# Weight sums, forms of x and squares in a two-MLP kernel: where the splits are made and what holds the buffers

## The chip, the cores and the metric

The kernel runs on one core of a Trainium2 chip. The metric is the device time of one execution in microseconds (us); before the change it is 1036.32 us, the median of two runs (1035.69 and 1036.94). The engines are named as in the profile: PE is TensorE (PEld its weight loads), DVE is VectorE, ACT is ScalarE, POOL is GpSimd and SP is SyncE, which only issues transfers here.

## What is computed

Sparse attention (half of the heads local, half strided), and then two MLPs one after the other, on 2304 tokens of 512 features:

```python
attn_out = _attn_ref(q, k, v)                       # 4 batches, 8 heads, 576 positions, 64 wide
x = transpose(attn_out).reshape(2304, 512)
h = x @ w_in;  r = np.maximum(h, 0.0)               # first MLP, 2048 wide
x = (s * (r * r) + b) @ w_out
a = x @ w2_a;  b2 = x @ w2_b                        # second MLP, 1536 wide
out = (a * b2) @ w2_out
```

Weights come as 64-bit words that have to be made float32 on the core.

## The kernel before

Every float32 operand is *split* into a high and a low half in a matmul format: ScalarE copies the high half, VectorE subtracts it from the value and writes the low one. Each product then is three matmuls (high by high, high by low, low by high).

**First MLP.** The tokens are taken in five blocks, n = 0 to 4, of 512, 384, 512, 384 and 512 columns. A block goes through 16 slices f of the hidden layer: h_mm makes h (12 matmuls), ScalarE writes r = relu(h) and squares it in place, split makes gt, and o_mm (12 matmuls) adds to the block's output, which leaves as o1s to DRAM at the block's end. The attention of the next block runs inside blocks 0 to 3.

**Second MLP.** It goes over the tokens in three pairs (0, 1, 2) of two 384-column blocks, and takes seven products instead of eight per 2 x 2 block of matrices. For this it needs sums and differences of the weight's quarters (s1 to s4 beside a11, a12, a22) and of x's quarters (the *forms* b11, b22, t1, t3, t2, b21, t4, two tiles each). A pair is 12 groups g of seven products (42 matmuls a group, "pp<-x2w,wf"), whose results become quads, and then a second-layer stage of 42 steps of six matmuls ("o<-gf,o2w"), where gf is the split of a quad's part.

**Work for the second MLP that lies elsewhere.** convert_w2 takes the 36 weight tiles through blocks 1 to 3: a load into raw, the conversion to w2s, a write of the whole tile to DRAM (w2d), splits of those quarters that need no sum, back into raw, and their writes to w2a, w2b and w2o from POOL's queue. raw is free again when that write has landed. sums(g) loads two such tiles again (w2r, four tiles), makes s1 to s4 (w2t), splits them (w2z, w2t) and writes them to w2s or w2o; there are 18, 15 of them emitted in block 4 and the last three within the first groups of pair 0. The forms of pair 0 are made in block 4 straight into the x2w tiles. Those of pairs 1 and 2 are made during the products of the pair before them, in two staging tiles (x2s), written to DRAM (x2d) from POOL's queue and copied back to x2w by SP in the second-layer stage.

**What sets the order.** Each engine runs its own instructions in program order, with what a scheduler has put there at build time. The helpers act and dve (L611 and L616) tie their calls into a chain on ScalarE and on VectorE. A transfer waits in its queue until its source is written and its destination is free, and those behind it in that queue wait too. SP's queue holds the loads wf (four per group, six tiles), w2r, o2w (eight tiles), xr and the copies x2w. Tiles of a pool come free with the last reader of their former contents.

Of the kernel before, what the change touches and what calls it, by code (L numbers as in the profile page):

```python
# [2 lines left out]

# [16 lines left out]
P = 128  # L20
# [6 lines left out]
def sparse_attention_two_mlps(  # L27
# [66 lines left out]
    FORMS = ("b11", "b22", "t1", "t3", "t2", "b21", "t4")  # L94
    x2d = [
        {name: [dram.tile([P, 2, TB2], F32, name=f"x2d{i}{name}{kk}") for kk in range(2)] for name in FORMS}
        for i in range(1, NP2)
    ]
# [38 lines left out]
    def to_float32(r, out=None, quarters=False):  # L137
# [12 lines left out]
        if quarters:  # L150
            to = out.rearrange("p (a i c) -> p a i c", a=2, c=STR)
            low, high = (t.rearrange("p (i a c) -> p a i c", a=2, c=STR) for t in (low, high))
            pieces_ = [(to[:, a], high[:, a], low[:, a]) for a in range(2)]
# [625 lines left out]
    def h_mm(n, f):  # L779
# [11 lines left out]
        with tc.high_priority(offset=URGENT):  # L791
            r = hp.tile([P, TM], F32, tag="r", name="r")[:, 0:T]
            relu = nc.scalar.activation(out=r, in_=ph, func=AF.Relu)  # L793
            gt = gp.tile([P, 2, TM], F32R, tag="gt", name="gt")
            hi, lo = gt[:, 0, 0:T], gt[:, 1, 0:T]
            nc.scalar.activation(out=r, in_=r, func=AF.Square)  # L796
            last = split(hi, lo, r)
            if n == 1:
                nc.scalar.activation(out=gt[:, :, T:T + 2], in_=bc, func=AF.Copy)
# [28 lines left out]
    def halves_of(w):  # L828
        return w.rearrange("p (a r c) -> p r a c", a=2, c=P)

    def convert_w2():
        words = {}
        for i in range(3 * NF2 + 1):
# [3 lines left out]
            if i:  # L837
                f, kind = divmod(i - 1, 3)
                with after(list(behind)):
                    r = words.pop(i - 1)  # L840
                    w = to_float32(r, hp.tile([P, DM], U32, tag="w", name="w2s"), kind == 2)
                    nc.gpsimd.dma_start(out=w2d[i - 1], in_=w)  # L842
                    z = r.rearrange("p c t -> p (c t)").bitcast(F32R)
                    if kind < 2 and f % 2 == 0:
                        z = z.rearrange("p (e c) -> p e c", e=2)
                        split(z[:, 0], z[:, 1], w)
                        to = w2a[f + kind]
                    elif kind < 2:
                        z = z[:, 0:DM].rearrange("p (e c) -> p e c", e=2)
                        split(z[:, 0], z[:, 1], w[:, HALF:])  # L850
                        to = w2b[f - 1 + kind]
                    elif f % 2 == 0:
                        z = z[:, 0:DM].rearrange("p (e a c) -> p e a c", e=2, a=2)
                        split(z[:, 0], z[:, 1], halves_of(w)[:, 0])
                        z = z.rearrange("p e a c -> p e (a c)")
                        to = w2o[f // 2][:, 0]
                    else:
                        z = z.rearrange("p (r e a c) -> p r e a c", r=2, e=2, a=2)
                        split(z[:, :, 0], z[:, :, 1], halves_of(w))
                        z = z.rearrange("p r e a c -> p r e (a c)")  # L860
                        to = w2o[f // 2][:, 1:3]
                    nc.gpsimd.dma_start(out=to, in_=z.bitcast(F32))
# [4 lines left out]
    NQ2 = NF2 // 2  # L867

    def sums(g, chained=False):
        if g < NG2:  # L870
            pair, kind = divmod(g, 2)
            first_, second = 6 * pair + kind, 6 * pair + 3 + kind
        else:
            first_, second = 6 * (g - NG2) + 2, 6 * (g - NG2) + 5
        r = [p2.tile([P, DM], F32, tag="r", name="w2r", bufs=4) for _ in range(2)]
        for t, i in zip(r, (first_, second)):
            nc.sync.dma_start(out=t, in_=w2d[i])
        yield
        t = p2.tile([P, 4, HALF], F32, tag="s", name="w2t", bufs=2)
        z = p2.tile([P, 4, HALF], F32R, tag="z", name="w2z")  # L880
        s2, s1, s3, s4 = (t[:, i] for i in range(4))
        vector = partial(dve, "tensor_tensor") if chained else nc.vector.tensor_tensor
        if g < NG2:
            a11, a12 = r[0][:, 0:HALF], r[0][:, HALF:]
            a21, a22 = r[1][:, 0:HALF], r[1][:, HALF:]
        else:
            a11, a21 = (halves_of(r[0])[:, i] for i in range(2))
            a12, a22 = (halves_of(r[1])[:, i] for i in range(2))
            s2, s1, s3, s4 = (i.rearrange("p (a c) -> p a c", a=2) for i in (s2, s1, s3, s4))
# [8 lines left out]
        for e, src in enumerate((z, low)):  # L898
            if g < NG2:
                nc.gpsimd.dma_start(out=w2s[g][:, :, e], in_=src.bitcast(F32).rearrange("p (i r) c -> p i (r c)", i=2))  # L900
            else:
                nc.gpsimd.dma_start(out=w2o[g - NG2][:, 3:, e], in_=src.bitcast(F32))  # L902
# [57 lines left out]
    def x2_forms(xr, pair):  # L960
        b11, b12, b21, b22 = (xr[:, c, 2 * r:2 * r + 2] for r in range(2) for c in range(2))

        def less(out_, in0, in1):
            dve("tensor_tensor", out=out_, in0=in0, in1=in1, op=ALU.subtract)
# [467 lines left out]
```

## Time and profile before

| what | us |
|---|---|
| median of two runs | 1036.32 |
| the profiled execution | 1035.28 |
| its span in the trace | 1033.6 |
| PE busy in it | 918.0 |
| DVE busy | 641.6 |
| ACT busy | 413.2 |
| POOL busy | 147.0 |
| moved by DMA | 241.33 MB |

The profile is of one execution. An engine is busy while it runs an instruction; waits for semaphores and the issue of transfers are not counted. Times within the trace run from the start of its span. The attention alone and the first blocks take up to 147 us, blocks 1 to 3 reach to about 428 us, block 4 to 523, pair 0 to 720, pair 1 to 894, pair 2 to the end.

### The profile page before, as it was taken

What the parts mean: (1) busy time and instruction counts of PE and PEld (TensorE: products, weight loads), DVE (VectorE), ACT (ScalarE), POOL (GpSimd) and SP (SyncE); (2) the same over time, 40 slices, a digit from 0 to 9 for tenths busy, and PEclk for the clock granted to TensorE, in tenths of its full rate; (3) what the DMA queues carried; (4) which work ended last, traced back from release to release, by engine and by line L of the source; (5) the groups of instructions that cost most, each with busy time, mean ns of one, the idle gap of its engine ahead of it and who ended that gap; (6) DMA issues with size and microseconds to landing.
All of it is one profiled execution on the core that took longest, in us unless ns stands there. A gap on an engine that the chain in (4) does not pass through costs nothing.

```text
span 1033.6 us, 17448 instructions
## 1 busy us (share of the span) xinstructions
PE 918.0 (89%) x6274; PEld 832.0 (80%) x6274; DVE 641.6 (62%) x1313; ACT 413.2 (40%) x876; POOL 147.0 (14%) x292
## 2 busy tenths in 40 slices
PE   8999999989798998999959965869996578999997
PEld 7778888977676888988848855859996578999997
DVE  6898955546565666368537644845555385465594
ACT  6777754545444545565422211322121133111251
POOL 5000001111111111022211011006101101500002
PEclk9999999989998999999979987989998898999999
DMA  9858436676767675479899766899776599877666
GB/s 247 233 165 222 103 113 185 183 185 203 198 196 195 215 218 183 157 246 306 283 374 356 271 219 219 289 348 288 248 251 212 211 331 308 276 248 249 197 210 198
DMA packets 206246, 241.33 MB, mean 233 GB/s; under 512 B 110992, under 2 KB 152528, under 8 KB 206160
## 3 DMA queue, kind: packets, MB, share of 16 engines
q1 hardware_dynamic: 184400, 181.88, 58.0%
q0 software_dynamic: 18048, 57.42, 15.2%
q10 hardware_dynamic: 3712, 0.92, 0.5%
q8 instruction: 50, 0.82, 0.4%
q14 instruction: 36, 0.29, 0.1%
HBM read 177.24 MB, written 62.91 MB: 232 GB/s over the span
## 4 chain that ended last, share of the span: by engine, by line
issue 44%; PE 33%; DMA 9%; POOL 8%; DVE 3%; ACT 2%; SPq 1%; POOLq 0%; ACTq 0%
PE o L103 10%; PE pp L103 9%; PE h L103 5%; PE acc L103 5%; DMA o2w<-w2o 3%; POOL w2s L900 2%; POOL w2d L842 1%; POOL out_dram L1254 1%; DMA w2b<-raw 1%; DVE quad L616 1%; DMA x2w<-x2d2t 1%; DMA x2w<-x2d1t 1%; POOL w2o L902 1%; DMA x2w<-x2d2b 1%; PE fpo L103 1%
## 5 line engine op out<-in xcount | busy, mean ns | idle before, releaser
L103 PE MATMUL pp<-x2w,wf 128*128 128x384 f32 x1512 | 288.3, 351 | 55.6 <-ACT quad L611 29.0
L103 PEld LDWEIGHTS pp<-x2w,wf 128*128 128x128 f32 x1512 | 277.8, 199 | 65.7 <-ACT quad L611 31.2
L103 PE MATMUL h<-x,w 128*128 128x512 f32 (+1 forms) x960 | 227.2, 387 | 10.5 <-ACT r L793 9.1
L103 PE MATMUL acc<-gt,w 128*128 128x512 f32 (+2 forms) x960 | 212.7, 370 | 2.7 <-ACT gt L120 1.4
L103 PEld LDWEIGHTS h<-x,w 128*128 128x128 f32 x960 | 178.8, 196 | 38.4 <-ACT r L793 11.7
L103 PEld LDWEIGHTS acc<-gt,w 128*128 128x128 f32 x960 | 176.5, 189 | 27.3 <-ACT gt L120 2.2
L103 PE MATMUL o<-gf,o2w 128*128 128x384 f32 x756 | 136.9, 342 | 24.6 <-DMA o2w<-w2o 24.0
L103 PEld LDWEIGHTS o<-gf,o2w 128*128 128x128 f32 x756 | 134.6, 192 | 26.5 <-issue 24.7
L121 DVE TENSOR_TENSOR gt<-r,gt 128x512 fp32r<-128x512 f32 (+1 forms) x80 | 50.9, 636 | 79.8 <-ACT gt L120 79.5
L616 DVE TENSOR_TENSOR quad<-pp,quad 128x384 f32<-128x384 f32 x108 | 59.9, 555 | 57.2 <-PE pp L103 53.0
L611 ACT ACTIVATE gf<-quad 128x384 fp32r<-128x384 f32 x126 | 62.1, 521 | 80.4 <-PE o L103 59.2
L616 DVE TENSOR_TENSOR gf<-quad,gf 128x384 fp32r<-128x384 f32 x126 | 65.6, 551 | 25.4 <-ACT gf L611 25.0
L1254 POOL DMA_DIRECT2D out_dram<-ot x84 | 47.2, 570 | 212.3 <-DVE ot L1241 210.0
L793 ACT ACTIVATE r<-h 128x512 f32<-128x512 f32 (+1 forms) x80 | 44.3, 554 | 78.4 <-PE h L103 64.3
L611 ACT ACTIVATE quad<-pp 128x384 f32<-128x384 f32 x36 | 17.6, 489 | 125.0 <-PE pp L103 120.1
L139 ACT ACTIVATE raw<-raw 128x512 f32<-128x512 f32 x66 | 43.1, 677 | 54.7 <-DMA raw<-in_moe_w_a_dram 22.0
L611 ACT ACTIVATE x2s<-xr 128x384 fp32r<-128x384 f32 x28 | 14.0, 520 | 94.8 <-DMA x2d2t<-x2s 19.4
L120 ACT ACTIVATE gt<-r 128x512 fp32r<-128x512 f32 (+1 forms) x80 | 47.0, 587 | 1.6
L842 POOL DMA_DIRECT2D w2d<-w2s x36 | 19.7, 547 | 192.7 <-DVE w2s L155 160.9
L796 ACT ACTIVATE r<-r 128x512 f32<-128x512 f32 (+1 forms) x80 | 46.7, 583 | 0.7
L616 DVE TENSOR_TENSOR x2s<-xr,x2s 128x384 fp32r<-128x384 f32 x28 | 15.5, 554 | 47.8 <-ACT x2s L611 47.8
L142 DVE TENSOR_SCALAR raw<-raw 128x512 uint32<-128x512 uint32 x66 | 26.8, 424 | 29.3 <-DMA raw<-in_moe_w_a_dram 17.7
(168 smaller groups left out, 885.0 us busy)
## 6 DMA issues: line engine op xcount, KB each, us to landing
wf<-w2s SPq DMA_DIRECT2D x72, 512.0 KB
o2w<-w2o SPq DMA_DIRECT2D x126, 256.0 KB
wf<-w2a SPq DMA_DIRECT2D x36, 512.0 KB
raw<-in_moe_w_out_dram SPq DMA_DIRECT2D x28, 512.0 KB
w2d<-w2s POOLq DMA_DIRECT2D x36, 256.0 KB, 3.1
w2r<-w2d SPq DMA_DIRECT2D x36, 256.0 KB
wf<-w2b SPq DMA_DIRECT2D x36, 256.0 KB
raw<-in_moe_w_in_dram SPq DMA_DIRECT2D x16, 512.0 KB
```

Of the source, the lines that this page charges most:

```text
L103: last_pe[:] = [nc.tensor.matmul(*args, **kwargs).ins]
L120: nc.scalar.activation(out=hi, in_=src, func=AF.Copy)
L121: return nc.vector.tensor_tensor(out=lo, in0=src, in1=hi.bitcast(F32), op=ALU.subtract)
L139: nc.scalar.activation(out=high.bitcast(F32), in_=high.bitcast(F32), func=AF.Copy, scale=HIGH_SCALE)
L142: nc.vector.tensor_scalar(out=low, in0=low, scalar1=29, scalar2=None, op0=ALU.logical_shift_right)
L611: i = nc.scalar.activation(**kwargs).ins
L616: i = getattr(nc.vector, method)(**kwargs).ins
L793: relu = nc.scalar.activation(out=r, in_=ph, func=AF.Relu)
L796: nc.scalar.activation(out=r, in_=r, func=AF.Square)
L842: nc.gpsimd.dma_start(out=w2d[i - 1], in_=w)
L900: nc.gpsimd.dma_start(out=w2s[g][:, :, e], in_=src.bitcast(F32).rearrange("p (i r) c -> p i (r c)", i=2))
L1254: engines[i % len(engines)].dma_start(out=at.rearrange("(j t) c -> t j c", t=STR), in_=st[i * STR:(i + 1) * STR, j:j + m].rearrange("t j a ...
```

## The change

1. convert_w2 converts and writes w2d only. The splits of the quarters and their 30 writes leave blocks 1 to 3.
2. sums makes them, in block 4 and pair 0: it splits the sums (w2t) and also the loaded tiles (w2r), the high halves into a new tile spare, the low ones in place, and issues six writes instead of two. Thirteen sums are emitted from f = 2 of block 4 on, one for each f, the others in groups 0 to 4 of pair 0.
3. In blocks 1 to 3 h_mm lets ScalarE square straight into the high half, while VectorE squares r itself and subtracts.
4. Forms of x are made straight in the x2w tiles for all pairs: in a pair one bias for each of groups 3 to 10 and the first difference in group 11, ten of the fourteen copies in the second-layer stage (one every fourth step), and the last four in the first group of the next pair. The staging tiles, x2d and the copies back are gone.
5. Homes: twelve tiles for gf instead of eleven, of which two forms per quad are made during the products and the others eleven steps ahead instead of nine; o2w has two tiles of its own, two in the first MLP's room hp and four in w2r's; the next pair's first four wf loads stand in the second-layer stage instead of in group 11; the quads come last in the order of pools.

```diff
@@ h_mm
-            nc.scalar.activation(out=r, in_=r, func=AF.Square)
-            last = split(hi, lo, r)
...
+            if n in (0, NB - 1):
+                nc.scalar.activation(out=r, in_=r, func=AF.Square)
+                last = split(hi, lo, r)
+            else:
+                nc.scalar.activation(out=hi, in_=r, func=AF.Square)
...
+                nc.vector.tensor_tensor(out=r, in0=r, in1=r, op=ALU.mult)
+                last = nc.vector.tensor_tensor(out=lo, in0=r, in1=hi.bitcast(F32), op=ALU.subtract)
@@ convert_w2
-                    r = words.pop(i - 1)
-                    w = to_float32(r, hp.tile([P, DM], U32, tag="w", name="w2s"), kind == 2)
-                    nc.gpsimd.dma_start(out=w2d[i - 1], in_=w)
-                    z = r.rearrange("p c t -> p (c t)").bitcast(F32R)
-                    if kind < 2 and f % 2 == 0:
-                        z = z.rearrange("p (e c) -> p e c", e=2)
-                        split(z[:, 0], z[:, 1], w)
-                        to = w2a[f + kind]
...
-                    nc.gpsimd.dma_start(out=to, in_=z.bitcast(F32))
+                    w = to_float32(words.pop(i - 1), hp.tile([P, DM], U32, tag="w", name="w2s"), kind == 2)
+                nc.gpsimd.dma_start(out=w2d[i - 1], in_=w)
@@ sums
+    EARLY = NF1 - 3
...
-        (act if chained else nc.scalar.activation)(out=z, in_=t, func=AF.Copy)
-        low = t.bitcast(F32R)
-        vector(out=low, in0=t, in1=z.bitcast(F32), op=ALU.subtract)
...
+        if own:
+            forms = [(flat(t), 2, w2s[g]), (r[0], 1, w2a[g][:, None]), (a22, 1, w2b[g][:, None])]
+        else:
+            to = w2o[g - NG2]
+            forms = [(flat(t), 4, to[:, 3:]), (r[1], 2, to[:, 1:3]), (a11, 1, to[:, 0:1])]
+        z = [room(0), room(1)]
+        z = [z[0], z[1][:, 0:DM], z[1][:, DM:DM + HALF]]
+        for high, (src, _, _) in zip(z, forms):
+            scalar(out=high, in_=src, func=AF.Copy)
+            vector(out=src.bitcast(F32R), in0=src, in1=high.bitcast(F32), op=ALU.subtract)
+        for high, (src, m, to) in zip(z, forms):
+            for e, half in enumerate((high.bitcast(F32), src)):
+                nc.gpsimd.dma_start(out=to[:, :, e], in_=half.rearrange("p (i c) -> p i c", i=m))
@@ x2_forms, form
-                if pair:
-                    w = p2.tile([P, 2, DM], F32R, tag="s", name="x2s", bufs=2)
-                else:
-                    w = slot(wpa, [P, 2, DM], "x2w", F32R)
-                    fixed.append(w)
+                if len(fixed) < 2:
+                    fixed.append(slot(wpa, [P, 2, DM], "x2w", F32R))
+                w = fixed[kk]
...
-                if pair:
-                    nc.gpsimd.dma_start(out=x2d[pair - 1][name][kk], in_=w[:, :, 0:TB2].bitcast(F32))
@@ block 4
-                    next(added[f])
-                    if f:
-                        next(added[f - 1])
+                    if 0 <= f - 2 < EARLY:
+                        next(added[f - 2])
+                    if f == 3:
+                        spare = xp[1].tile([P, 3, 2 * DM], F32R, tag="x", name="spare")
+                    if 0 <= f - 3 < EARLY:
+                        next(added[f - 3])
@@ pools of the second MLP
-    gq, wf, tmp, rp, op = pool("gq", NQ2), pool("wf", 4), pool("tmp", 6), pool("rp", 8), pool("op", 4)
+    rp, op, wf, tmp, gq = pool("rp", 9), pool("op", 2), pool("wf", 4), pool("tmp", 6), pool("gq", NQ2)
@@ pair, groups
-                for _ in range(2):
-                    next(later_x[0], None)
-            elif later_x:
-                next(later_x[1], None)
+            if later_x and 3 <= g < 11:
+                next(later_x[0])
+            if later_x and g == 11:
+                next(later_x[1])
...
-            if pair == 0 and g + NF1 <= NG2 + NQ2:
-                if g + NF1 < NG2 + NQ2:
-                    next(added[g + NF1])
-                next(added[g + NF1 - 1])
+            j = EARLY + g
+            if pair == 0 and j < NG2 + NQ2:
+                if j + 1 < NG2 + NQ2:
+                    next(added[j + 1])
+                next(added[j])
@@ second-layer stage
-            if i >= 2 and copies:
-                name, kk = copies.pop(0)
-                nc.sync.dma_start(out=x2[name][kk][:, :, 0:TB2].bitcast(F32), in_=x2d[pair][name][kk])
+            if not last:
+                if i % 4 == 2 and 8 <= i < 24:
+                    next_room()
+                if i % 4 == 3:
+                    next(later_x[1])
```

**How the instructions move.** The first place is ScalarE in a middle block, where raw is the second MLP's weight in conversion, r and gt are the first MLP's hidden values. Before:

```order
L139 ACTIVATE raw<-raw 128x512
L796 ACTIVATE r<-r 128x512
L120 ACTIVATE gt<-r 128x512
L120 ACTIVATE x<-po 128x128 x2
L120 ACTIVATE raw<-w2s 128x2x256
L793 ACTIVATE r<-h 128x512
L139 ACTIVATE raw<-raw 128x512
L796 ACTIVATE r<-r 128x512
L120 ACTIVATE gt<-r 128x512
L120 ACTIVATE raw<-w2s 128x512
```

ScalarE in a middle block after the change:

```order
L135 ACTIVATE raw<-raw 128x512
L796 ACTIVATE gt<-r 128x512
L789 ACTIVATE r<-h 128x512
L135 ACTIVATE raw<-raw 128x512
L796 ACTIVATE gt<-r 128x512
L482 ACTIVATE pT<-ppt 128x256
```

The copies raw<-w2s are gone, and one instruction, gt<-r, stands where two stood.

The second place is the start of pair 0's products, on ScalarE (quad and u are the copies that TensorE waits for, w2z and spare the high halves of weights). Before:

```order
L820 ACTIVATE o1s<-acc,sb 128x512 x2
L895 ACTIVATE w2z<-w2t 128x1024
L611 ACTIVATE quad<-pp 128x384 x2
L611 ACTIVATE w2z<-w2t 128x1024
L611 ACTIVATE u<-pp 128x384
L611 ACTIVATE w2z<-w2t 128x1024
L611 ACTIVATE quad<-pp 128x384 x2
```

ScalarE at the start of pair 0's products after the change:

```order
L607 ACTIVATE quad<-pp 128x384 x2
L873 ACTIVATE spare<-w2t 128x1024
L873 ACTIVATE spare<-w2r 128x512
L873 ACTIVATE spare<-w2r 128x256
L873 ACTIVATE spare<-w2r 128x512
L873 ACTIVATE spare<-w2r 128x256
L873 ACTIVATE spare<-w2t 128x1024 x2
L873 ACTIVATE spare<-w2r 128x512
L873 ACTIVATE spare<-w2r 128x256
L607 ACTIVATE spare<-w2t 128x1024
L607 ACTIVATE gf<-w2r 128x512
L607 ACTIVATE gf<-w2r 128x256
```

The next row there is u<-pp of group 1: the splits of four sums stand ahead of it now (gf<-w2r is a high half in a tile that gf gets later). SP's queue in groups 1 and 2 after the change (w2s_167 holds the sums of group 2, its first load s2 and s1, its second s3 and s4):

```order
L908 DMA wf<-w2s_167 128x1024
L908 DMA wf<-w2b_155 128x2x256
L852 DMA w2r<-w2d_136 128x512
L852 DMA w2r<-w2d_139 128x512
L852 DMA w2r<-w2d_107 128x512
L852 DMA w2r<-w2d_110 128x512
L852 DMA w2r<-w2d_113 128x512
L852 DMA w2r<-w2d_116 128x512
L852 DMA w2r<-w2d_119 128x512
L852 DMA w2r<-w2d_122 128x512
L1180 DMA o2w<-w2o_177 128x512
L908 DMA wf<-w2s_167 128x1024
```

Before, two w2r loads stood among the wf loads of these groups; now the eight loads of four sums stand ahead of the second load of group 2.

The third place is SP's queue in pair 0's second-layer stage. Before:

```order
L1398 DMA x2w<-x2d1t_187 128x2x384
L933 DMA wf<-w2s_165 128x1024
L1398 DMA x2w<-x2d1t_188 128x2x384
L933 DMA wf<-w2a_142 128x1024
L1398 DMA x2w<-x2d1b_185 128x2x384
L933 DMA wf<-w2s_166 128x1024
L1398 DMA x2w<-x2d1b_186 128x2x384
L1210 DMA o2w<-w2o_179 128x512
L1398 DMA x2w<-x2d1t_195 128x2x384
L1210 DMA o2w<-w2o_180 128x512
```

SP's queue in pair 0's second-layer stage after the change:

```order
L908 DMA wf<-w2b_153 128x2x256
L908 DMA wf<-w2s_165 128x1024
L908 DMA wf<-w2a_142 128x1024
L908 DMA wf<-w2s_166 128x1024
L1180 DMA o2w<-w2o_179 128x512
L1180 DMA o2w<-w2o_180 128x512
L1180 DMA o2w<-w2o_181 128x512
```

The copies x2w<-x2d are gone from between the loads.

## Rows read from the trace of the kernel before

**Rows 1.** Windows of the second MLP; columns from start to GB/s as headed.

```profile
core 0: us, PE busy (x) PEld busy (x) DVE busy (x) ACT busy (x) POOL busy (x), PEclk, DMA share, GB/s
523.00:660.00 137.00, 102.82 (x508) 97.50 (x507) 70.41 (x133) 28.39 (x56) 15.50 (x22) 0.88 0.79 279
660.00:720.00 60.00, 46.33 (x254) 45.16 (x253) 35.90 (x69) 17.12 (x35) 14.10 (x26) 0.91 0.98 334
720.00:837.00 117.00, 96.00 (x503) 93.07 (x502) 62.14 (x118) 23.98 (x51) 17.47 (x29) 0.93 0.70 233
837.00:894.00 57.00, 46.13 (x255) 45.84 (x255) 36.28 (x70) 17.13 (x35) 13.08 (x24) 0.91 0.96 324
894.00:983.00 89.00, 88.55 (x504) 86.74 (x503) 52.44 (x99) 13.53 (x29) 5.01 (x9) 1.00 0.70 232
983.00:1034.00 51.00, 44.66 (x255) 43.87 (x253) 36.85 (x74) 17.05 (x35) 6.99 (x12) 0.97 0.71 207
```

**Rows 2.** Timeline of PE, its last matmuls: start, us, what.

```profile
1023.80 3.89 PE L103 MATMUL o<-gf,o2w 128*128 128x384 f32 x21
```

**Rows 3.** Waits of PE in pair 0's products, 523 to 660: total, times, longest.

```profile
PE pp L103 <- ACT quad L611: 19.3, 4, 8.6
PE pp L103 <- ACT u L611: 11.5, 3, 5.8
```

**Rows 4.** Waits of PE in pair 1's products, 720 to 837.

```profile
PE pp L103 <- ACT u L611: 10.8, 2, 6.1
PE pp L103 <- ACT quad L611: 9.7, 2, 5.0
```

**Rows 5.** Timeline of ACT in pair 0's products; in brackets the idle time ahead.

```profile
643.99 0.52 ACT L611 ACTIVATE x2s<-xr 128x384 fp32r<-128x384 f32 x1 [9.11 <-DMA x2d1t<-x2s]
644.41 0.47 ACT L611 ACTIVATE quad<-pp 128x384 f32<-128x384 f32 x1
```

**Rows 6.** Waits of PE in pair 0's second-layer stage, 660 to 720.

```profile
PE o L103 <- DMA o2w<-w2o: 13.1, 3, 11.2
```

**Rows 7.** Waits of PE in pair 1's second-layer stage, 837 to 894.

```profile
PE o L103 <- DMA o2w<-w2o: 10.9, 1, 10.9
```

**Rows 8.** Timeline of SP's queue as pair 0's second-layer stage begins.

```profile
659.80 4.01 SPq L1398 DMA_DIRECT2D x2w<-x2d1t  x3
```

**Rows 9.** Windows: blocks 1 to 3, the last block, pair 0's start.

```profile
147.00:428.00 281.00, 258.21 (x2571) 228.09 (x2569) 166.67 (x396) 135.57 (x300) 40.92 (x74) 0.95 0.66 192
444.00:523.00 79.00, 77.31 (x337) 62.82 (x337) 57.32 (x106) 44.74 (x70) 19.34 (x28) 1.00 0.86 286
525.00:575.00 50.00, 36.75 (x179) 34.03 (x179) 26.05 (x49) 11.67 (x20) 6.03 (x8) 0.86 1.02 376
```

**Rows 10.** Waits of PE in the middle blocks, 120 to 440.

```profile
PE h L103 <- ACT r L793: 9.1, 5, 3.7
PE po L103 <- issue: 5.8, 3, 2.8
```

**Rows 11.** Waits of ACT in the middle blocks, 130 to 428.

```profile
ACT raw L120 <- DVE w2s L155: 37.0, 21, 3.5
ACT raw L139 <- DMA raw<-in_moe_w_a_dram: 22.0, 7, 7.1
```

**Rows 12.** Groups of DVE's instructions by form, 130 to 430: total, mean ns.

```profile
L121 DVE TENSOR_TENSOR raw<-w2s,raw 128x512 fp32r<-128x512 f32 x18 | 12.4, 689 | 9.3 <-ACT raw L120 9.3
```

**Rows 13.** Groups of DVE's instructions in the last block, 428 to 523.

```profile
L897 DVE TENSOR_TENSOR w2t<-w2t,w2z 128x1024 fp32r<-128x1024 f32 x14 | 17.1, 1223 | 16.3 <-ACT w2z L895 16.3
L894 DVE TENSOR_TENSOR w2t<-w2r 128x256 f32<-128x256 f32 x30 | 11.4, 421 | 4.2 <-DMA w2s<-w2t 4.1
```

**Rows 14.** Transfers issued from 445 to 523: count, size, us to landing.

```profile
w2s<-w2t POOLq DMA_DIRECT2D x12, 512.0 KB, 4.6
```

**Rows 15.** Transfers issued from 523 to 600.

```profile
w2o<-w2t POOLq DMA_DIRECT2D x4, 512.0 KB, 8.5
```

**Rows 16.** Timeline of ACT at the start of pair 0.

```profile
527.46 1.06 ACT L895 ACTIVATE w2z<-w2t 128x1024 fp32r<-128x1024 f32 x1 [3.94 <-DMA w2o<-w2z]
```

**Rows 17.** Groups of POOL's instructions, 428 to 600.

```profile
L900 POOL DMA_DIRECT2D w2s<-w2t x12 | 8.3, 690 | 10.8 <-DVE w2t L897 10.8
```

More of the change, by code (lines that the diff above doesn't have):

```diff
@@ L2 @@
 from functools import partial
+from itertools import cycle
 import concourse.bass as bass
@@ L867, in sparse_attention_two_mlps, with sums @@
     NQ2 = NF2 // 2
[L869 to L874, printed above, removed]
+    EARLY = NF1 - 3
+    def sums(g, room, vector, scalar):
+        own = g < NG2
+        first_ = 6 * (g // 2) + g % 2 if own else 6 * (g - NG2) + 2
         r = [p2.tile([P, DM], F32, tag="r", name="w2r", bufs=4) for _ in range(2)]
-        for t, i in zip(r, (first_, second)):
+        for t, i in zip(r, (first_, first_ + 3)):
             nc.sync.dma_start(out=t, in_=w2d[i])
         yield
+        quarter = lambda t, i: t[:, i * HALF:(i + 1) * HALF]
+        a11, a22 = quarter(r[0], 0), quarter(r[1], 1)
+        a12, a21 = (quarter(r[0], 1), quarter(r[1], 0)) if own else (quarter(r[1], 0), quarter(r[0], 1))
         t = p2.tile([P, 4, HALF], F32, tag="s", name="w2t", bufs=2)
-        z = p2.tile([P, 4, HALF], F32R, tag="z", name="w2z")
         s2, s1, s3, s4 = (t[:, i] for i in range(4))
[L882 to L889, printed above, removed]
         for out_, in0, in1, op in (
@@ L894, in sums @@
             vector(out=out_, in0=in0, in1=in1, op=op)
-        (act if chained else nc.scalar.activation)(out=z, in_=t, func=AF.Copy)
-        low = t.bitcast(F32R)
-        vector(out=low, in0=t, in1=z.bitcast(F32), op=ALU.subtract)
[L898 to L902, printed above, removed]
+        flat = lambda t: t.rearrange("p i c -> p (i c)")
+        if own:
[11 more added lines that the diff above has]
+                nc.gpsimd.dma_start(out=to[:, :, e], in_=half.rearrange("p (i c) -> p i c", i=m))
         yield
@@ L958, in x2_bias, with x2_forms, less @@
                 yield
[L960 removed]
+    def x2_forms(xr):
         b11, b12, b21, b22 = (xr[:, c, 2 * r:2 * r + 2] for r in range(2) for c in range(2))
[L963 to L964 removed]
+        def less(out_, in0, in1, op=ALU.subtract):
+            dve("tensor_tensor", out=out_, in0=in0, in1=in1, op=op)
         def form(name, src):
@@ L1126, in sparse_attention_two_mlps @@
             xr = x2_load(0)
-            ahead = [x2_bias(xr), x2_forms(xr, 0)]
-            added = [sums(g, g >= NF1 - 1) for g in range(NG2 + NQ2)]
+            ahead = [x2_bias(xr), x2_forms(xr)]
+            spares = cycle(range(3))
+            added = [
+                sums(g, lambda i: spare[:, next(spares)], nc.vector.tensor_tensor, nc.scalar.activation)
+                for g in range(EARLY)
+            ]
         for f in range(NF1):
@@ L1299, in sparse_attention_two_mlps @@
         next_room()
+    spare = p2.tile([P, 2 * DM], F32R, tag="z", name="spare")
+    spares = cycle([rings[i].rearrange("p e c -> p (e c)") for i in (NR - 2, NR - 1)])
+    added += [
+        sums(g, lambda i: next(spares) if i else spare, partial(dve, "tensor_tensor"), act)
+        for g in range(EARLY, NG2 + NQ2)
+    ]
+    next(added[EARLY])
     sets = [[ps_acc.tile([P, TM], F32, tag="acc", name="o2")[:, 0:TB2] for _ in range(2)] for _ in range(2)]
@@ L1373, in sparse_attention_two_mlps @@
         engines = (nc.sync, nc.scalar) if last else (nc.gpsimd,)
-        sums_, made = {}, NQ2
-        copies = [(name, kk) for name in FORMS for kk in range(2)] if not last else []
-        def make(upto):
-            nonlocal made
-            while made < min(upto, len(order2)):
-                n, fp = order2[made]
-                g_form(quads, n, fp)
+        sums_, made = {}, 2 * NQ2
+        for i, (n, fp) in enumerate(order2):
+            while made < min(i + NR - 1, len(order2)):
+                g_form(pair, quads, made)
                 made += 1
-        for i, (n, fp) in enumerate(order2):
-            make(i + 9)
             if fp == 0 and n:
```

113 lines of the change are left out of this document (45 added, 68 removed).

## The prediction

> **What bounds the kernel now.** I began with the busy times by stage, because what a change is worth is read in its own stage. In the second MLP [rows 1] two of three pairs run slowly. Pair 2 does its 504 product matmuls in 89 us at clock 1.00; pair 0 takes 137 us and pair 1 117 us for the same matmuls, at 0.88 and 0.93. The second-layer stage of pair 2 lasts from 983.0 to 1027.7 by its last matmul [rows 2], 44.7 us; the other two take 60 and 57 us. So the losses are 48.0, 15.3, 28.0 and 12.3, together 104 us. Pair 2 is the floor in the same execution: it has neither weight sums nor forms of x beside it.
>
> Next the waits of TensorE there. In the products it waits almost only for ScalarE's copies quad and u: 30.8 us in pair 0 [rows 3], 20.5 us in pair 1 [rows 4]. ScalarE is busy for 28 of 137 us, so something holds its queue. Its timeline shows what [rows 5]: the copy x2s, half of a form of the next pair's x, waits 9.11 us for a write of an earlier form to land, and the quad copy that TensorE needs runs right behind it. In the second-layer stages TensorE waits for o2w, 13.1 and 10.9 us [rows 6, 7], whose loads stand behind the x2w copies in SP's queue; three of these in a row take 4.01 us to issue [rows 8].
>
> Last the middle blocks. From 147 to 428 us TensorE is busy for 258.2 of 281 us, at a mean clock of 0.95 [rows 9]: 22.8 us idle, and about 258.2 x 0.05 = 12.9 us spent at the lower of its two levels, 1.2 GHz, behind idle times: 35.7 us in all. The first wait there is that of h for ScalarE's r [rows 10], and ScalarE waits for raw loads and for the conversions whose halves it makes [rows 11].
>
> **The change part by part, against the profiled execution's 1035.3 us** (its span of 1033.6 and 1.7 around it; 1.0 under the median of the runs).
>
> *Blocks 1 to 3.* 36 splits leave. On VectorE that is 18 x 0.689 [rows 12] + 18 x 0.421 (the row for 256 columns, [rows 13]) = 20.0 us, on ScalarE a similar time, and 30 writes leave POOL. A raw tile is free after its conversion and no longer after a landing, so its next load starts earlier. Against it VectorE squares r 48 times, at most 48 x 0.689 = 33 us, since two of the three blocks have 384 columns instead of 512. VectorE is then up by at most 13 us in 281, of which it is busy for 166.7; ScalarE loses 48 squares. Of the idle time 5.8 us (po<-issue in [rows 10]) is no wait for these engines, so three quarters of 22.8 hangs on late ScalarE or VectorE work. Three quarters of 35.7 is 26.8; less 3.8 for r x r, which now stands between h and o, I take **-23**. Bounds: 0, if VectorE takes ScalarE's place, and -33.
>
> *The last block.* A sum moves 2.36 MB instead of 1.57 and has three splits instead of one; VectorE's share of the new ones is 0.69 + 0.42 us. From 444 to 523 us the trace moves 22.6 MB at 286 GB/s [rows 9]; 14 sums are 22.0 of it. Ten sums, which is what the order places in this block, are 23.6 MB, with what else moves about 25 MB, or 316 GB/s; 376 was reached over 50 us [rows 9], so there is room. But r<-h stands behind the sums' splits in ScalarE's queue, and a split waits for a tile whose landing can be late. **+4** (0 to +20: five pairs of sums at 8.5 instead of 4.6 us to a landing, [rows 14, 15]).
>
> *Pair 0's products.* Eight sums fall here instead of four. ScalarE has splits of four of them between quad of group 0 and u of group 1. SP has the loads of four sums ahead of the load that holds s3 and s4 of group 2; each waits until a w2r tile has been written out, and behind it wait all later wf loads. That is a new wait, and TensorE waits for both. By bytes: 8 x 2.36 + 6 groups x 1.84 = 29.9 MB at 376 GB/s is 80 us, where six groups need 6 x 89 / 12 = 44.5. By latency: a sum is a load, four adds of 0.42, splits, six POOL issues and a landing. With 8.5 us for either transfer [rows 15], splits of 1.06 [rows 16] + 1.22 [rows 13] + 0.69 + 0.42 and issues of 6 x 0.69 [rows 17] that is 26.2 us; the four w2r tiles hold two sums, so 13.1 us a sum, 105 us for eight. With 4.6 us [rows 14] it is 18.4 / 2 = 9.2, 74 us, and the bytes bind. I take 8 us over the bytes, since landings still come between: 87.5 us, 10.9 a sum. That is a loss of 43, where the whole of pair 0 lost 48, and the other six groups run at pair 2's pace, as no form of x waits there any more: **-5** (-13 to +13, from the bytes alone and from the long landings).
>
> One page speaks against the rate in it. The Trainium skill, "DMA: Bandwidth & Descriptors", section Specifications, gives a limit of about 358 GB/s of HBM per core. The trace went above it, 376 GB/s over 50 us [rows 9], so I go by the trace. By the page the bytes would take 84 us instead of 80, this term would be -1, and the sum 969.
>
> *Forms of x.* 28 writes and 28 loads of 384 KB leave, and with them the waits of [rows 5] and the queue ahead of o2w. One bias a group stays in the products, less than before. Pair 1's products lost 28.0; its first group now holds the last four copies of the forms, which can cost a wait of ScalarE: **-26** (-20 to -28), and **+1.5** for the same four copies at the start of pair 2 (0 to 4). Into the two inner second-layer stages come ten copies on ScalarE, which is busy for 17 of 51 us there, and on VectorE ten low halves and three wide differences. VectorE was busy for 36.85 us in pair 2's stage [rows 1]; plus 10 x 0.52 (384 columns, three quarters of 0.689) + 3 x 0.92 (768, three quarters of 1.22), less six low halves of gf that are now made earlier (3.1), that is 41.8 of 44.7 us. The work hides, if barely, since gf now runs eleven steps ahead instead of nine. So **-13** of 15.3 and **-10** of 12.3 (each up to 5 less, if VectorE is late).
>
> Sum: -23 + 4 - 5 - 26 + 1.5 - 13 - 10 = -71.5; 1035.3 - 71.5 = 963.8 profiled, 965 as a median.
>
> **The rivals.**
> *VectorE takes ScalarE's place in the middle.* It stands once more between h and o in each f. For it: up to 33 us of new work. Against it: VectorE is busy for 59% of that stretch. The middle then gains nothing: 965 + 23 = 988.
> *The sums pace more than forecast, two at a time.* The last block at its bound (+16) and pair 0 at 13.1 us a sum (+17): 965 + 33 = 998. For it: in just this stretch landings took 8.5 us [rows 15], and a split waited 3.94 us for one [rows 16].
> *The sums run one at a time,* the other side. If the load of a sum stands in SP's queue behind a wf load that waits for a product, while that product's u waits for the sum before, the four tiles no longer overlap: 26.2 us a sum. Pair 0 then takes 8 x 26.2 + 44.5 = 254 us instead of 132, and the time is 1087. It is no gain from (132 + 71.5 - 44.5) / 8 = 19.9 us a sum on, and 2% slower from 22.4. For it: the order has such a place, in groups 1 and 2. Against it: the later sums stand one to a group.
> *VectorE becomes the bound in the second-layer stages.* At 41.8 of 44.7 us any wait for ScalarE's half of a form adds to it; 5 us in each stage give 975.
> *The forms no longer wait, and another wait ends the stalls at the same time,* so that this part doesn't do what it says: the stalls would come from busy DMA queues and not from x2s. For it: pair 0's products have a DMA share of 0.79. Against it: pair 1's have 0.70, as pair 2's, which don't stall. If pair 1 and the two stages kept two thirds of their loss, it would be 965 + 33 = 998, and 1021 if the middle gave nothing either.
>
> **How the numbers follow.** The forecast, with every term inside its bounds, 940 to 985: 0.60. VectorE in the middle: 0.12. Sums two at a time: 0.10. VectorE in the second-layer stages: 0.06. Another wait for the forms': 0.06, a third of it above 1015. Sums one at a time: 0.06, a sixth of it within 2%. Faster by over 2% (below 1015.6; about what a measurement of this kernel can tell from no change) is 0.60 + 0.12 + 0.10 + 0.06 + 0.04 = 0.92, less 0.02 for two of these at once: 0.90. Within 2%: 0.05. Slower: 0.05. The range for 8 in 10 reaches from 935 (the middle and pair 0 both near their lower bounds) to 1002, past the rivals at 988 and 998; the likeliest case alone is 940 to 985.
>
> **What would show it.** Pair 1's products at 91 us or less and at clock 1.00, with no wait of ScalarE for a landing; the two inner second-layer stages at 45 to 48 us, without a wait for o2w; pair 0's products at about 132 us, with the loss in the first six groups and TensorE waiting for u, quad or wf behind a write-out of a sum; the stretch of the middle blocks at 258 us instead of 281, with no raw load that waits for a write. The prediction is wrong if pair 0's products pass 150 us, if the last block stretches by over 10 us, or if TensorE waits for gt's low half in the middle as long as it now waits for r.

## The result, and the profile after

The changed kernel takes 968.99 us (median of two runs, 968.67 and 969.31) against 1036.32 before: a ratio of 0.935 with a 95% interval of 0.931 to 0.939, so 6.5% faster. The forecast was 965, with 935 to 1002 for 8 in 10. The profiled execution took 968.67 us.

The sum came out almost as forecast, but two of its terms did not. Stage by stage, from the two profiled executions (blocks 1 to 3 are taken from the first output copy of block 0, o1s, to the first of block 3, the last block from there to pair 0's first product, a later stage from its first matmul to that of the next):

| stage | before, us | after, us | change | forecast |
|---|---|---|---|---|
| blocks 1 to 3 | 296.9 | 260.5 | -36.4 | -23 (0 to -33) |
| last block | 83.6 | 85.3 | +1.7 | +4 |
| pair 0, products | 136.6 | 149.3 | +12.7 | -5 (-13 to +13) |
| pair 0, second layer | 60.1 | 47.4 | -12.7 | -13 |
| pair 1, products | 117.4 | 94.9 | -22.5 | -26 |
| pair 1, second layer | 56.7 | 45.9 | -10.8 | -10 |
| pair 2, products | 89.4 | 90.6 | +1.2 | +1.5 |

Windows of the changed kernel (length, then busy time and count of PE, PEld, DVE, ACT and POOL, granted clock, DMA share, GB/s): blocks 1 to 3, the first 96 us of pair 0, the rest of its products, and then its second layer, pair 1's products and second layer, and pair 2's products. They answer to [rows 1, 9].

```profile
147.00:392.00 245.00, 243.82 (x2572) 218.15 (x2571) 172.95 (x405) 95.01 (x218) 21.18 (x38) 1.00 0.62 163
489.00:585.00 96.00, 47.33 (x222) 44.83 (x220) 51.12 (x98) 23.27 (x43) 31.60 (x49) 0.77 0.97 352
585.00:638.00 53.00, 51.60 (x282) 50.24 (x283) 33.65 (x64) 11.08 (x23) 3.43 (x6) 0.97 0.81 262
638.00:685.50 47.50, 45.70 (x255) 45.41 (x254) 39.72 (x78) 20.15 (x45) 15.14 (x28) 0.96 0.84 266
685.50:780.50 95.00, 91.04 (x506) 88.58 (x505) 57.70 (x110) 19.77 (x41) 6.94 (x13) 0.98 0.75 250
780.50:826.20 45.70, 43.90 (x254) 43.61 (x252) 39.27 (x77) 20.05 (x45) 13.10 (x24) 1.00 0.86 275
826.20:917.00 90.80, 89.26 (x506) 87.37 (x506) 57.22 (x109) 15.73 (x33) 4.96 (x9) 1.00 0.69 227
```

The middle is full: TensorE is busy for 243.8 of 245 us at clock 1.00, where [rows 9] had 258.2 of 281 at 0.95. What is left of the loss stands in one place, the first 96 us of pair 0: 222 matmuls where pair 2's pace (504 in 89 us) would make about 540, at a DMA share of 0.97. After that pair 0 runs near that pace, 282 matmuls in 53 us.

The timeline of PE there (in brackets the idle time ahead):

```profile
488.75 3.63 PE L99 MATMUL pp<-x2w,wf 128*128 128x384 f32 x18
505.60 8.53 PE L99 MATMUL pp<-x2w,wf 128*128 128x384 f32 x36 [13.21 <-DMA wf<-w2s]
534.35 8.96 PE L99 MATMUL pp<-x2w,wf 128*128 128x384 f32 x42 [20.23 <-ACT u L607]
```

Of ACT, whose copy u ends the second wait, and of SP's queue:

```profile
519.46 0.94 ACT L873 ACTIVATE spare<-w2r 128x512 fp32r<-128x512 f32 x2 [19.68 <-DMA w2r<-w2d]
533.83 0.47 ACT L607 ACTIVATE u<-pp 128x384 f32<-128x384 f32 x1
```

```profile
498.13 0.54 SPq L908 DMA_DIRECT2D wf<-w2b  x1
509.81 0.33 SPq L908 DMA_DIRECT2D wf<-w2s  x1
513.11 0.52 SPq L908 DMA_DIRECT2D wf<-w2b  x1
513.73 22.74 SPq L852 DMA_DIRECT2D w2r<-w2d  x8
```

This is the place that the order showed: the wf load of 509.81 waits for a tile that a product frees, TensorE's 13.2 us delay that product, and the loads of four sums stand behind it until 513.73. ScalarE then waits 19.7 us for the first of them, with u of group 1 behind.

### The profile page after: what moved, and what is told of

Read it like the earlier page. It is cut to its first block, busy times and chain, and to the rows that moved or that the text cites. A ratio compares the mean times of both kernels' runs of the same rounds, so it can differ in the third digit from the quotient of the medians.

```text
span 967.0 us, 17286 instructions
## 1 busy us (share of the span) xinstructions
PE 893.1 (92%) x6274; PEld 815.2 (84%) x6274; DVE 664.2 (69%) x1361; ACT 383.8 (40%) x828; POOL 149.9 (15%) x300
## 3 DMA queue, kind: packets, MB, share of 16 engines
q0 software_dynamic: 15488, 46.41, 13.2%
## 4 chain that ended last, share of the span: by engine, by line
PE 69%; DVE 9%; issue 7%; DMA 6%; ACT 3%; POOL 3%; SPq 1%; DVEq 0%; POOLq 0%; ACTq 0%
PE h L99 19%; PE pp L99 19%; PE acc L99 18%; PE o L99 8%; DVE quad L612 3%; DVE gf L612 2%; DMA wf<-w2s 2%; PE po L99 2%; DMA out_dram<-ot 1%; DMA w2o<-w2r 1%; PE pss L99 1%; POOL w2o L877 1%; PE ppt L102 1%; DVE ot L1211 1%; POOL out_dram L1224 1%
## 5 line engine op out<-in xcount | busy, mean ns | idle before, releaser
L99 PE MATMUL pp<-x2w,wf 128*128 128x384 f32 x1512 | 279.7, 344 | 55.6 <-ACT u L607 26.6
L99 PEld LDWEIGHTS pp<-x2w,wf 128*128 128x128 f32 x1512 | 271.1, 194 | 63.9 <-ACT u L607 27.6
L99 PE MATMUL h<-x,w 128*128 128x512 f32 (+1 forms) x960 | 218.8, 376 | 3.5 <-ACT r L789 3.5
L99 PEld LDWEIGHTS h<-x,w 128*128 128x128 f32 x960 | 172.8, 189 | 28.8 <-ACT r L789 4.2
L612 DVE TENSOR_TENSOR quad<-pp,quad 128x384 f32<-128x384 f32 x108 | 59.9, 554 | 45.9 <-PE pp L99 45.5
L607 ACT ACTIVATE quad<-pp 128x384 f32<-128x384 f32 x36 | 17.7, 491 | 134.4 <-PE pp L99 134.4
L799 DVE TENSOR_TENSOR r<-r 128x384 f32<-128x384 f32 (+1 forms) x48 | 28.9, 603 | 58.9 <-ACT gt L796 58.9
L839 POOL DMA_DIRECT2D w2d<-w2s x36 | 19.7, 547 | 208.2 <-DVE w2s L151 193.6
L141 DVE SCALAR_TENSOR_TENSOR raw<-raw 128x512 uint32<-128x512 uint32 x66 | 44.3, 687 | 0.7
L612 DVE TENSOR_TENSOR quad<-quad 128x384 f32<-128x384 f32 x72 | 40.0, 556 | 2.0
L117 DVE TENSOR_TENSOR gt<-r,gt 128x512 fp32r<-128x512 f32 x32 | 22.0, 689 | 25.5 <-ACT gt L116 25.5
L612 DVE TENSOR_TENSOR u<-pp,u 128x384 f32<-128x384 f32 x36 | 19.9, 554 | 24.2 <-PE pp L99 24.2
L612 DVE TENSOR_TENSOR x2w<-xr,x2w 128x384 fp32r<-128x384 f32 x42 | 22.9, 550 | 14.7 <-ACT x2w L607 14.7
```

Of the source, the lines that this page charges most:

```text
L99: last_pe[:] = [nc.tensor.matmul(*args, **kwargs).ins]
L117: return nc.vector.tensor_tensor(out=lo, in0=src, in1=hi.bitcast(F32), op=ALU.subtract)
L141: nc.vector.scalar_tensor_tensor(out=low, in0=high, scalar=3, in1=low, op0=ALU.logical_shift_left, op1=ALU.bitwise_or)
L607: i = nc.scalar.activation(**kwargs).ins
L612: i = getattr(nc.vector, method)(**kwargs).ins
L799: nc.vector.tensor_tensor(out=r, in0=r, in1=r, op=ALU.mult)
```

## The experiments

Each was run beside the kernel before on the same chip (medians of 1031 to 1037 us there, so ratios are compared, not times). Stages are read from each profile, here from a stage's first matmul to the end of its last one, which is up to 0.2 us more than in the table.

**The forms of x alone.** x2_forms, its calls and the stage that copied back, as in the change; all else is the kernel before:

```diff
-                if pair:
-                    w = p2.tile([P, 2, DM], F32R, tag="s", name="x2s", bufs=2)
...
+                if len(fixed) < 2:
+                    fixed.append(slot(wpa, [P, 2, DM], "x2w", F32R))
+                w = fixed[kk]
```

> Before, with only the forms of x made in place (the staging tiles, their writes and the copies back gone, no other part of the change). Theory (two staging tiles held until a write lands stop ScalarE, and the copies back stand ahead of o2w): pair 1's products fall from 117 to about 93 us, the two inner second-layer stages from 60 and 57 to 46 to 48 us, and the second half of pair 0's products (596 to 660, which lost 28 us) runs at pair 2's pace, so that pair 0's products take about 110 us; in all about -75, 961 us. Rival (the stalls come from busy DMA queues): pair 1's products stay above 108 us and the whole above 1010 us.

959.92 us, ratio 0.931 (0.923 to 0.939). Pair 0's products take 110.6 us, pair 1's 96.2, the inner second-layer stages 48.3 each. The theory holds, and more follows than was expected: this one part gives as much as the whole change (0.935). Some 9 us of it in this profile are none of its doing: blocks 1 to 3 take 287.7 us instead of 296.9, with the same instructions in the same order on every engine, and 295.3 in the last version below, which leaves them alone too. So that stretch can differ by 9 us between two profiles with nothing changed in it.

The run takes away three things at once: the hold of the staging tiles, the copies' places in SP's queue, and 22 MB of traffic (219.3 MB in all against 241.3). In the products the waits for landings are seen directly [rows 5], and pair 1 had no higher DMA share than pair 2, which does not stall [rows 1]. In the second-layer stages, place and bytes are not separated. Before, TensorE did the first eight steps of pair 0's stage from loads issued ahead and waited for the ninth. That load was issued 10.9 us after the stage's start, among the copies, and TensorE went on 8.8 us later, in a stretch in which the core moved 385 GB/s:

```profile
670.54 0.33 SPq L1210 DMA_DIRECT2D o2w<-w2o  x1
679.35 3.96 PE L103 MATMUL o<-gf,o2w 128*128 128x384 f32 x12 [11.19 <-DMA o2w<-w2o]
660.00:680.00 20.00, 8.81 (x50) 8.52 (x49) 15.86 (x31) 4.41 (x10) 0.00 (x0) 0.82 1.06 385
```

**The change without it.** The staging tiles, writes and copies back are put back into the changed kernel:

```diff
-                if len(fixed) < 2:
-                    fixed.append(slot(wpa, [P, 2, DM], "x2w", F32R))
-                w = fixed[kk]
+                if pair:
+                    w = p2.tile([P, 2, DM], F32R, tag="s", name="x2s", bufs=2)
...
+                    nc.gpsimd.dma_start(out=x2d[pair - 1][name][kk], in_=w[:, :, 0:TB2].bitcast(F32))
```

> The changed kernel with the forms of x of pairs 1 and 2 staged, written and copied back as before. Theory (staging tiles and copies back): pair 1's products return to about 115 us, the inner second-layer stages to about 57 us each, pair 0's products to 160 us or more; the whole at about 1025 us (1012 to 1045). Rival (busy queues, which the smaller number of weight tiles has eased by itself): below 990 us.

1043.56 us, ratio 1.012 (1.006 to 1.018), about what was expected: pair 1's products are back at 120.5 us, the second-layer stages at 61.4 and 58.7, pair 0's products at 176.6. The waits of ACT in pair 1's products are those of [rows 5] again (total, times, longest):

```profile
ACT x2s L613 <- DMA x2d2t<-x2s: 20.1, 3, 10.9
ACT x2s L613 <- DMA x2d2b<-x2s: 12.3, 3, 7.3
```

With the forms in place, in the changed kernel, ACT waits only for other engines there, mostly for products that are not done:

```profile
ACT quad L607 <- PE pp L99: 53.3, 12, 8.7
ACT u L607 <- PE pp L99: 15.0, 6, 5.2
ACT gf L607 <- DVE quad L612: 11.3, 6, 2.2
```

So beside staged forms all other parts together made the kernel slower by about 1%, although blocks 1 to 3 take 36.8 us less than before in this run too.

**raw no longer held.** In the kernel before, the writes of the halves read a constant tile of the first MLP's weights:

```diff
-                    nc.gpsimd.dma_start(out=to, in_=z.bitcast(F32))
+                    nc.gpsimd.dma_start(out=to, in_=other)
```

> Before, where the 30 writes of the halves in blocks 1 to 3 read a constant tile of the first MLP's weights instead of raw (the second MLP's weights are wrong by that; splits, writes and bytes stay as many). Theory (raw held until its halves have landed makes the next load late): the stretch of blocks 1 to 3 falls from 281 to about 255 us, the whole to about 1010 us, though all splits are still made there. Rival (it is the splits' work on ScalarE and VectorE that is in the way): the stretch stays at 272 us or more, the whole at 1027 or more.

1033.73 us, ratio 1.002 (0.999 to 1.005): inconclusive. Nothing tied these writes to their places any more, and they ran at 37 to 60 us, where TensorE lost 25 us in block 0; blocks 1 to 3 themselves took 265.2 us. The writes were then tied to the write of w2d ahead of each:

```diff
+                    with after([first.ins]):
+                        nc.gpsimd.dma_start(out=to, in_=other)
```

> Before, where the 30 writes of halves in blocks 1 to 3 read a constant tile of the first MLP's weights instead of raw, each now ordered behind the write of w2d of its own tile, so that they stay at their places (the second MLP's weights are wrong by that; splits, writes and bytes stay as many). From the last output copy of block 0 to the first of block 3 it is 296.9 us before and 260.5 us with the change. Theory (raw held until its halves have landed): 265 us or less, the whole about 1002 us. Rival (the splits' work or the writes' traffic): 285 us or more, the whole 1020 us or more.

1008.30 us, ratio 0.975 (0.971 to 0.978). The stretch falls to 265.7 us (it and the two figures in the expectation start at the first output copy of block 0, not the last). The window and the groups of ACT in it (total, mean ns, idle time before):

```profile
147.00:397.00 250.00, 245.25 (x2573) 218.44 (x2571) 165.08 (x396) 133.55 (x300) 39.98 (x74) 1.00 0.76 217
```

```profile
L120 ACT ACTIVATE raw<-w2s 128x512 fp32r<-128x512 f32 (+1 forms) x36 | 18.8, 522 | 46.7 <-DVE w2s L155 46.7
```

All 36 splits are there, 18.8 us of ScalarE, with all their writes (one a tile, so 36 and not the 30 that the change and the expectations speak of), and TensorE is full at clock 1.00. Before, SP's loads of raw waited 87 us in all for writes from raw to land, most of it in these two rows (total, times, longest):

```profile
SPq L127 <- DMA w2o<-raw: 44.3, 7, 8.7
SPq L127 <- DMA w2a<-raw: 14.3, 4, 5.9
```

So what held the middle up was raw waiting for its landings, and neither the splits' work nor the writes' traffic: 31 of the 36 us, or 22 against the 287.7 us that the same instructions took in the run above. One thing is not separated from it: with the hold gone, the build also put the instructions of ScalarE, VectorE and SP in another order there. And since pair 0's sums stay small here (138.6 us for its products), these 31 us reach the end nearly whole: 26 us.

**The square back on ScalarE** in the changed kernel, in blocks 1 to 3:

```diff
-            if n in (0, NB - 1):
+            if n >= 0:
```

> The changed kernel with the square of r made by ScalarE in blocks 1 to 3 as before. Theory (the splits and raw's landings made the middle late, the square only moves work): the stretch of blocks 1 to 3 stays at 245 to 250 us, the whole at 969 to 974 us. Rival (moving the square carries the gain in the middle): the stretch is 260 us or more, the whole 984 us or more.

967.98 us, ratio 0.939 (0.931 to 0.946), and 259.8 us for the middle stretch: nothing changed. Moving the square neither helps nor costs.

**The loads of the sums from POOL's queue:**

```diff
-            nc.sync.dma_start(out=t, in_=w2d[i])
+            nc.gpsimd.dma_start(out=t, in_=w2d[i])
```

> The changed kernel with the loads of w2r issued from POOL's queue instead of SP's. Theory (in pair 0's first groups the loads of a sum stand behind wf loads that wait for products, and u of group 1 waits for that sum): the waits of 13 and 20 us at the start of pair 0 shrink by about 15 us together, pair 0's products from 149 to about 134 us, the whole to about 953 us. Rival (bytes and landings pace the sums, whatever queue loads them): pair 0's products at 145 us or more.

975.97 us, ratio 0.944 (0.937 to 0.950); pair 0's products take 162.1 us, with waits of 15.1 and 29.1 us at their start. Against the theory: the loads left SP's queue and the wait for u grew, now behind write-outs in POOL's queue. Taking them out of SP's queue does not pay by itself; a queue in which nothing stands ahead of them was not tried.

**Ten sums early instead of thirteen:**

```diff
-    EARLY = NF1 - 3
+    EARLY = NF1 - 6
```

> The changed kernel with ten sums emitted in the last block instead of thirteen, and the other eight one for each of groups 0 to 7. Only one split set then stands ahead of u of group 1 and one pair of w2r loads between wf loads. Theory (the crowding of four sums ahead of u of group 1): by bytes eight groups of 4.2 MB at 376 GB/s are 89 us, four more 30 us; pair 0's products about 122 to 132 us, the whole about 945 us. Rival (bytes and landings pace them): 145 us or more.

962.32 us, ratio 0.930 (0.925 to 0.936). Pair 0's products take 141.8 us: the wait of 20 us for u goes down to 1.3, but waits of up to 7.5 us appear in later groups. Between the two theories: the crowding accounts for 8 us of pair 0's loss.

**Only w_out's splits behind the sums.** convert_w2 splits w_a and w_b as before:

```diff
-            forms = [(flat(t), 2, w2s[g]), (r[0], 1, w2a[g][:, None]), (a22, 1, w2b[g][:, None])]
+            forms = [(flat(t), 2, w2s[g])]
```

> The changed kernel, where only the splits of w_out's tiles go behind the sums and those of w_a and w_b stay in the conversion in blocks 1 to 3 (24 of the 36 splits, 24 of the 30 tiles' writes). Twelve sums are small again (1.57 MB). Theory (each landing that holds raw costs in the middle, and the bytes of the sums cost in pair 0): the middle from 260 to about 280 us, pair 0's products from 149 to about 118 us; the whole about 957 us. Rivals: the middle does not come back at all (260: the landings of w_out's halves alone held it), the whole about 940 us; or it comes back wholly (297), the whole about 975 us.

958.67 us, ratio 0.927 (0.922 to 0.931); 279.6 us in the middle, 123.1 in pair 0's products. About half of the middle's gain is kept and about two thirds of what pair 0 pays is saved.

**The load of xr later.** In the changed kernel, in the one with ten sums early, and in the one with only w_out's splits moved (there with the six w_out sums in groups 1, 2, 4, 5, 7 and 8):

```diff
-                xr = x2_load(pair + 1)
+                with after(list(last_fill)):
+                    xr = x2_load(pair + 1)
```

> The changed kernel with one transfer moved: the load of pair 1's x (xr, 1.57 MB), which the queue issues as pair 0 begins, goes behind the wf loads of group 3. In the changed kernel the first 96 us of pair 0 move 33.8 MB at a DMA share of 0.97, and TensorE first waits 13.2 us for a wf load. Theory (bytes bind there, and this load is ahead of that wf load): the first wait falls to about 9 us, pair 0's products from 149 to about 145 us or somewhat less, the whole to about 964 us. Rival (the order of sums alone sets it): first wait and pair 0's products within 1 us of the changed kernel's.

> The changed kernel with ten sums in the last block, one in each of groups 0 to 7, and the load of xr behind the wf loads of group 3. Theory (bytes bind, and what can be moved to later groups, where DMA has room, is won): pair 0's products from 142, with ten sums early alone, to about 136 us, the whole about 955 us. Rival (the xr load is hidden anyway): 142 us and 961 us.

> The changed kernel, where only w_out's splits are behind the sums, its six sums go to groups 1, 2, 4, 5, 7 and 8 of pair 0, and the load of xr goes behind the wf loads of group 3. Theory (bytes bind in the first six groups): pair 0's products from 123, with only w_out's splits there, to about 112 us, the middle at 280 us as there; the whole about 946 us. Rival (the first groups' waits come from the transition itself, o1s and the first wf loads): 120 us or more, the whole 955 us or more.

969.03 us (0.938, 0.932 to 0.944), 957.73 us (0.927, 0.921 to 0.933) and 957.61 us (0.927, 0.923 to 0.932). In all three the first wait for wf falls, from 13.2 to 8.3, from 12.6 to 8.1 and from 11.6 to 5.6 us, and in none do pair 0's products follow: 153.1, 140.9 and 126.5 us against 149.3, 141.8 and 123.1. In its place a longer wait stands some groups later: 8.9 us for wf, 9.6 us for u and 5.1 us for wf.

**A version from what these show:** the forms in place, the splits left where they were, the change's order of pools for the quads, and xr and the first o2w loads behind wf loads.

```diff
-    gq, wf, tmp, rp, op = pool("gq", NQ2), pool("wf", 4), pool("tmp", 6), pool("rp", 8), pool("op", 4)
+    rp, op, wf, tmp, gq = pool("rp", 8), pool("op", 4), pool("wf", 4), pool("tmp", 6), pool("gq", NQ2)
```

> Before, with the forms of x made in place (as in the run with that part alone), the quads last in the order of pools as in the change, and two kinds of loads kept behind wf loads in SP's queue: xr behind those of group 3, the first eight o2w loads behind those of group 11. All splits stay in blocks 1 to 3. With the forms alone pair 0's products began at 511.5 us and ended at 622.0, with a first wait of 10.8 us for quad behind the landing of o1s. Theory (at pair 0's start bytes bind, and the order of pools makes quad wait for o1s): the first wait falls below 5 us, pair 0's products from 110.5 to about 102 us, the whole from 960 to about 951 us. Rival (the waits move on to the next load in the queue): pair 0's products 108 us or more, the whole 957 us or more.

957.14 us, ratio 0.924 (0.921 to 0.927): faster than the change by about 1%, with none of its work on the weights. Against the theory, pair 0's products take 111.2 us, as with the forms alone (110.6). The wait for quad fell from 10.8 to 3.3 us and one for wf took its place:

```profile
518.93 2.27 PE L103 MATMUL pp<-x2w,wf 128*128 128x384 f32 x12
524.47 1.32 PE L103 MATMUL pp<-x2w,wf 128*128 128x384 f32 x6 [3.27 <-ACT quad L611]
534.25 9.00 PE L103 MATMUL pp<-x2w,wf 128*128 128x384 f32 x36 [8.46 <-DMA wf<-w2s]
```

**What pair 0 pays for.** The windows of pair 0's products, of the kernels with the forms alone, only w_out's splits, ten sums early, xr later, and the loads on POOL, in that order:

```profile
511.50:622.00 110.50, 93.34 (x506) 89.33 (x506) 62.33 (x118) 21.90 (x42) 6.02 (x8) 0.94 0.84 303
```

```profile
503.30:626.30 123.00, 96.31 (x506) 92.23 (x505) 73.74 (x141) 28.00 (x54) 23.09 (x34) 0.92 0.93 329
```

```profile
489.70:631.40 141.70, 100.68 (x506) 94.20 (x505) 84.12 (x162) 34.05 (x65) 35.04 (x54) 0.88 0.94 337
```

```profile
486.30:639.30 153.00, 101.71 (x506) 97.14 (x505) 86.61 (x167) 35.15 (x65) 35.06 (x54) 0.82 0.89 313
```

```profile
484.00:646.00 162.00, 99.49 (x506) 95.22 (x505) 88.94 (x170) 37.04 (x68) 49.06 (x79) 0.81 0.89 315
```

Length times rate gives 33.5, 40.5, 47.8, 47.9 and 51.0 MB. From the first to the third, all at shares of 0.84 to 0.94, 14.3 MB more cost 31.2 us: 2.2 us for each MB. That would be a rate of 458 GB/s, more than the 352 to 385 GB/s of the full stretches shown here, so part of these bytes went into time that DMA had free. At about the same 48 MB the order of sums and loads makes 141.7, 149.3 (the change) or 153 us. So of the 38.7 us by which pair 0's products are longer in the change than with the forms alone, about 31 go with the bytes and about 8 with the order. That the bytes cause it is argued from this series, since each of these kernels also differs in its order; it was not shown alone.

## Why the prediction was right, and where it was not

**The forms of x** went as worked out: -12.7, -22.5, -10.8 and +1.2 us against -13, -26, -10 and +1.5, and the two runs with and without this part show that it carries them; whether the copies' places or their bytes held o2w up stays open. The 4.01 us of [rows 8] were read as issue time, but a single copy takes 0.52 us to issue in that queue, and the rest of the row lies between the issues. VectorE was reckoned at 41.8 us in the second-layer stages and is busy for 39.7; the work hides. Pair 1's products missed the sign that the prediction set, 91 us or less at clock 1.00. The 22.5 against 26 is two waits at their start: 1.1 us for VectorE behind the late forms, and 2.4 us for wf at 705.00, with the matmuls between at a lower clock (0.98 over the window).

**Blocks 1 to 3** gained 36.4 where -23 was taken, beyond the bound of -33. The mechanism was right, as the run with raw not held shows. Two steps of the term were wrong in size. The 5.8 us of po<-issue [rows 10] were kept out as no wait for these engines; they are gone with the rest (in the changed kernel the one wait of PE left in these blocks is 1.2 us), so they were late work all the same. And 3.8 us were charged for the square on VectorE, which costs next to nothing: put back, it changes the stretch by 0.7 us. The full 35.7 us that [rows 9] gave, idle time and clock, was the right figure for this execution of the kernel before (the 12.9 us in it are what the lower clock level cost, about half of the time spent at it). Against the 287.7 us that the same blocks took with the forms alone, the gain is 27 us.

**Pair 0's products** lost 12.7 us where -5 was taken, at the edge of the bound, and their 149.3 us lie just under the 150 past which the prediction called itself wrong. The step that failed is the sum of bytes. It counted 29.9 MB, eight sums and six groups' wf, and 80 us at 376 GB/s. The trace moves 33.8 MB in 96 us, at 352 GB/s, and only 5.3 groups are done by then: writes of the last block's sums, o1s, xr and the first o2w loads were left out, and the rate of 376 was that of a short stretch. The Trainium skill, "DMA: Bandwidth & Descriptors", section Specifications, puts the limit of a core at about 358 GB/s, as half of what two cores share. Over this longer stretch the trace lies nearer to that than to the 376 that was preferred, though single fortieths of it reach 422 GB/s; as this kernel runs on one core, no run here shows that this limit is what binds. The place where the order binds, sums behind wf loads and u behind sums, was named in advance and is where the 20.2 us wait stands. The pace of the sums themselves was right: the last write of the eighth is issued by 573.7, 85 us after the start, where 87.5 were taken:

```profile
572.45 1.28 POOL L877 DMA_DIRECT2D w2o<-w2r  x2
587.14 1.28 POOL L877 DMA_DIRECT2D w2o<-w2r  x2
```

But the second row is the end of a ninth: only nine of the 18 sums, and not ten, had issued their writes when pair 0 began. And about 4.5 groups of products were done by 573.7, and not six; the groups behind ran into two more waits and a lower clock.

**The rest.** The last block was +1.7 for +4. The errors in the middle (13.4 us more gain) and in pair 0 (17.7 us less) nearly cancelled, which is why 965 met 969; to that extent the total came out by luck. The prediction had put 24 of its 71.5 us on the weights and the square; the runs show that these parts together are at best neutral: what blocks 1 to 3 gain is given back in pair 0. The 14 MB that left there (54.1 MB in the window of [rows 9], 39.9 in that of the changed kernel) come back in pair 0's products (47.8 MB against 33.5 with the forms alone), where the queues were already full; that they are the cause is argued, as said above.

## What to carry to other kernels

Before moving work out of one stage, add up all bytes of the stage that receives it, with what earlier stages still have in flight and the loads that a queue issues early, at the rate of a stretch as long as the stage. A buffer that is free only when a write has landed can hold an engine that is idle 80% of the time; test such a hold by letting the write read something else, at its own place in the queue. Price each part of a change by a run with that part alone: here one of three parts carried all of the gain.

## What the runs showed of the hardware

In the kernel before, loads of raw waited in SP's queue until the writes that read raw had landed, up to 8.7 us at a time, and TensorE's mean clock over blocks 1 to 3 was 0.95; with the writes reading another tile it was 1.00, at a higher DMA share (0.76 against 0.66). Moving the loads of the sums to another issuing engine did not shorten pair 0 but made it longer (162.1 us from POOL, 149.3 from SP), as they then stood behind write-outs. Over 96 us at a share of 0.97 the core moved 352 GB/s, while 50 us of the kernel before had moved 376 GB/s at 1.02 [rows 9].
